# Half loads in 4 KB pieces, early weights behind the last load, a fourth place for outgoing rows: one change to a linear-attention and mixture-of-experts kernel

## The chip, the cores and the metric

The kernel runs on one NeuronCore of one Trainium2 chip. A core has a matrix engine (TensorE, PE in the profile, with its weight loads as PEld), a vector engine (VectorE, DVE), a scalar engine (ScalarE, ACT), a general engine (GpSimd, POOL) and a queue processor without arithmetic (SyncE, SP). Sixteen DMA engines move data between the chip's memory and the core's on-chip memory; SP, ACT and POOL each hand them transfers from a queue of their own, and each of these engines takes its instructions strictly in order. The metric is the device time of one execution in microseconds (us), lower is better.

## The reference

Two stages. The first is linear attention with decay over 4 batches, 8 heads, 768 positions and head dimension 64, with a state carried from block to block. Its output, 3072 token rows of 512, goes to a mixture of experts with one expert of eight for each token.

```python
def _attn_ref(q, k, v, lam):
    ...
    for b in range(nb):
        sl = slice(b * block, (b + 1) * block)
        qb, kb, vb = (q[:, :, sl], k[:, :, sl], v[:, :, sl])
        intra = np.einsum('bhic,bhjc->bhij', qb, kb) * Dmask[None]
        intra = np.einsum('bhij,bhjd->bhid', intra, vb)
        inter = np.einsum('bhid,bhde->bhie', qb * lam_pow[None], kv_state)
        out[:, :, sl] = intra + inter
        kb_dec = kb * rev_pow[None]
        kv_state = lam_block[None, :, None, None] * kv_state + np.einsum('bhsd,bhse->bhde', kb_dec, vb)

def _moe_ref(x, modality_id, w_gate, modality_bias, w1, w2):
    ...
    logits = x @ w_gate + modality_bias[modality_id]
    e_idx = np.argmax(logits, axis=1)
    ...
    for e in range(E):
        mask = e_idx == e
        h = np.maximum(x[mask] @ w1[e], 0.0)
        out[mask] = gate_w[mask, None] * (h @ w2[e])
    return out.astype(np.float32)
```

## The kernel before

**Attention.** The 768 positions of a batch are cut into 6 chunks of 128, so there are 24 chunks (`NC` = 6, `B` = 4). Two chunks make a half (`HB` = 2): one load of 2 MB brings keys and queries by columns, and values and keys by rows, for both chunks and all heads (`load_half`, L177). There are 12 halves and three buffers for them (`LOADS`). On the host `qkv` is laid out so that everything one partition needs of a half is one run of 16 KB (L882). The first half is loaded as four parts (L68, L90), the decay tables `dk` between them (L84, both from SP), so that chunk 0 can begin.

The loop over `g` (L696) is a pipeline written by hand. In round `g` stand: the scaled queries and keys of chunk g+1 (`prepare`, DVE, L200 and L205), the scores of chunk g (PE L220, masked on DVE at L223), the outputs of chunk g-1 (PE L258 and L269), the state update of chunk g (PE L235) and the token rows of chunk g-2 (`tokens`, L274: PE L281 turns them, ACT L282 copies them into `xn`, ACT's queue stores `xn` to the memory tensor `xs` at L283, DVE L285 sums the router's logits). `xn` has three places, so the copy of chunk n waits until the store of chunk n-3 has landed. A half's load is handed over in round g when the buffer of three halves before is free, that is after the outputs of that half's second chunk.

**Routing.** After each batch DVE ranks the tokens (`route`, `route_places`), and POOL scatters their numbers into the list `inv` (`write_slots`, L355), one write of 128 entries for each chunk. From the first two batches (`SOON`) two tiles of 256 tokens are chosen early (`early_list`, called at g = `early` = 14, with a matmul at L365 that needs the token count `ohsum`). Their list entries are read at g = 18 (`fetch_idx`, L500, waits until the scatters have landed), and their weights `raw1` (`fetch_w1`, L525) and `raw2` (`fetch_w2`, L531) follow in rounds 18 and 20, in four pieces of 512 KB each, all on SP's queue.

**Experts.** A wide tile has 256 tokens; weights, rows and hidden values are split into a high and a low part (`split`, L482 on ACT and L483 on DVE) and multiplied in three products (L548 to L552). A thin tile has 64 tokens and is computed unsplit (L578, L600). The order is: early tile 0 (`run(0)`), early tile 1 with both thin tiles (`run_early(1)`), then ten wide tiles. A weight load carries a condition: when the expert is that of the tile before, SP hands it over, but it moves nothing. In `run(0)` the number and place of all later tiles are worked out once the last tokens are routed (`late_list`); SP then reads register values and list entries of the later tiles (`get_idx`), and the second early tile's `raw2` comes after those in SP's order (L796). In `run_early` the rows of the first later wide tile are turned (`turn_rows`, L541) between the turns and products of the thin tiles.

**What sets the order.** The program's order is the basis, and a planner places the instructions of each engine by its own estimate of time. `behind(later, first)` adds a wait, with `wait=False` only an order. SP takes everything in turn: a register load or transfer that waits holds up all that stands behind it.

Of the kernel before, what the change touches and what calls it, by code (L numbers as in the profile page):

```python
# [6 lines left out]
F32 = mybir.dt.float32  # L7
# [8 lines left out]
P = 128  # L16
B, H, S, D = 4, 8, 768, 64
NP = H // 2
NC = S // P
HB = 2  # L20
LOADS = 3
N = B * S
E, DM, F = 8, 512, 1024
KC, FC = DM // P, F // P
TT = 256
# [13 lines left out]
def linear_attention_moe(tc, qkv, lam, modality, wg, mbias, w1, w2, out):  # L39
    nc = tc.nc  # L40
    with ExitStack() as ctx:
# [10 lines left out]
        def behind(later, first, wait=True):  # L52

            info = (mybir.DependencyInfo(mybir.DependencyClass.Sync, mybir.DependencyReason.DATA) if wait else
                    mybir.DependencyInfo(mybir.DependencyClass.NoSync, mybir.DependencyReason.SCHED_ONLY))
            tc.add_manual_dep(later.ins, first.ins.name, info, reason="order")
# [4 lines left out]

        def load_tile():

            return work.tile([P, HB, 4, H * D], F32, name="load", bufs=LOADS)

        first = load_tile()
        for part in (slice(0, 2), slice(2, 4)):
            nc.sync.dma_start(out=first[:, 0, part], in_=qkv[0, 0][:, 0, part])  # L68
        busy = const.tile([P, DM], BF16, name="busy")
        nc.vector.memset(busy, 0.0)  # L70
        tab = const.tile([H, 2 * P], F32, name="tab")
# [9 lines left out]

        dk = const.tile([P, 2, NP, P], F32, name="dk")
        for hl in range(2):
            tables = nc.sync.dma_start(  # L84
                out=dk[:, hl],
                in_=bass.AP(tensor=tab_d.tensor, offset=tab_d.offset + hl * 2 * P,
                            ap=[[1, P], [4 * P, NP], [1, P]]),
            )
        for part in (slice(0, 2), slice(2, 4)):
            ld = nc.sync.dma_start(out=first[:, 1, part], in_=qkv[0, 0][:, 1, part])  # L90
            behind(ld, tables, wait=False)
            tables = ld

# [81 lines left out]
        nc.vector.memset(ohsum, 0.0)  # L175

        def load_half(g):  # L177
            b, h = divmod(g, NC // HB)
            t = load_tile()
            behind(nc.sync.dma_start(out=t, in_=qkv[b, h]), tables, wait=False)  # L180
            return t

        halves = {0: first}

        def loaded(g):

            t = halves[g // HB][:, g % HB]
            kt, qt = (t[:, i].rearrange("p (a t) -> p a t", a=NP) for i in range(2))
            return kt, qt, t[:, 2], t[:, 3]

# [82 lines left out]

        def tokens(g, xt, lg):  # L274
            c = g % NC
            xn = work.tile([P, NP, P + E], F32, name="xn", bufs=3)
            for hf in range(2):
                xp = ps.tile([P, 2, 256], F32, name="x", bufs=2)
                for j in range(2):
                    p = hf * 2 + j  # L280
                    nc.tensor.matmul(xp[:, j, : P + E], xt[:, p, :], iw[:, p, :], start=True, stop=True)  # L281
                copies.append(nc.scalar.copy(out=xn[:, 2 * hf : 2 * hf + 2, :], in_=xp[:, :, : P + E]))  # L282
            nc.scalar.dma_start(out=xs[g * P : (g + 1) * P, :].rearrange("t (p d) -> t p d", p=NP),  # L283
                                in_=xn[:, :, :P])
            logits.append(nc.vector.tensor_reduce(out=lg[:, c, :], in_=xn[:, :, P:].rearrange("p q e -> p e q"),  # L285
                                                  axis=AX, op=ALU.add))
# [204 lines left out]
        def item(lst, row, i):  # L491
            return lst[0:1, row, i : i + 1] if isinstance(i, int) else lst[0:1, row, i]

        def fetch_idx(lst, i, idx, cols=TT):
            vr = nc.sync.value_load(item(lst, 1, i), min_val=0, max_val=E * CAP)
            if cols < TT:
                for p in range(0, P, cols):
                    nc.sync.dma_start(out=idx[p : p + cols, 0, :], in_=inv[bass.ds(vr, cols), 0:2])
                return
            nc.sync.dma_start(out=idx, in_=inv[bass.ds(vr, TT), 0:2].rearrange("(t p) c -> p t c", t=2))  # L500

        def groups(cols):

# [28 lines left out]
                if after is not None:  # L532
                    behind(ld, after)

        def turn_rows(cols, before=None):
            for i in range(2):
                tp = ps.tile([P, 2, TT], F32, name="x", bufs=2)
                for j in range(2):
                    kc = 2 * i + j
                    for t, m in groups(cols):  # L540
                        mm = nc.tensor.transpose(out=tp[:, j, t * P : t * P + m],  # L541
                                                 in_=xg[t][:m, kc * P : (kc + 1) * P], identity=ident[:m, :m])
                        if before is not None:
                            behind(mm, before, wait=False)
                split(tp[:, :, :cols], xh[i][:, :, :cols], xl[i][:, :, :cols])
# [150 lines left out]
        for g in range(0, ng + 2):  # L696
            if 1 <= g < ng - 1:
                st0[g + 1] = prepare(g + 1)
            if g == 2:
                routing_constants()  # L700
            if g < ng:
                st1[g], masked = scores(g)
            if g == 0:
                spread_powers()
                keep_busy(14)
                behind(nc.sync.dma_start(out=iw[:, :, P:], in_=wg), tables, wait=False)
                for i in range(1, LOADS):
                    halves[i] = load_half(i)
                for i in range(2):
                    st0[i] = prepare(i, masked)  # L710
            if 1 <= g <= ng:
                st2[g - 1], passed = outputs(g - 1, st1.pop(g - 1), from_state(g - 1, st0[g - 1][0]))
            if g < ng:
                passed = carry(g, st0[g][1]) or passed

            if g >= HB and g % HB == 0 and LOADS - 1 + g // HB < ng // HB:
                halves[LOADS - 1 + g // HB] = load_half(LOADS - 1 + g // HB)
            if g >= 2:
                b, c = divmod(g - 2, NC)
                if c == 0:  # L720
                    lgs[b] = work.tile([P, NC, E], F32, name="lg", bufs=2)
                tokens(g - 2, st2.pop(g - 2), lgs[b])
                if routed is not None:
                    slots = route_places(*routed)
                    routed = None
                if c == NC - 1:
                    routed = (b, *route(b, lgs.pop(b)))

            few = 2 if early <= g < early + 3 else 1
            write_slots(slots[:few], passed)  # L730
            slots = slots[few:]

            if g == early:
                exA, nA = early_list()
                er, _ = fetch_regs(listA, 0, True)
            elif g == early + 4:
                for i in range(EARLY):
                    fetch_idx(listA, i, idxA[i])
                fetch_w1(er, {})
            elif g == early + 6:  # L740
                fetch_w2(er, {})
            elif g == ng - 2:
                fetch_rows(idxA[0], TT, SOON * S, after=fades[-1])
            elif g == ng:
                split(raw1[0], w1h[0], w1l[0], late=True)
                turn_rows(TT)
            elif g == ng + 1:
                for i in range(1, 4):
                    split(raw1[i], w1h[i], w1l[i], late=True)
                fetch_w1(*fetch_regs(listA, 1, False))  # L750
                fetch_rows(idxA[1], TT, SOON * S)
# [11 lines left out]
        def regs(n):  # L763
            return fetch_regs(*tiles[n][1:], False)
# [21 lines left out]
        def run(n):  # L786
            idx = idxs.get(n) or get_idx(n)
            begun, turned = wide(tail, before)
            if n == 0:
                write_slots(route_places(*routed, begun))  # L790
                late_list(exA, nA)
            if n + 1 < fixed_ones:
                ahead = range(EARLY, wides + 1) if n == 0 else range(n + 2, min(n + 3, fixed_ones))
                for m in ahead:
                    idxs[m] = get_idx(m)
                fetch_w2(*regs(n + 1))  # L796
                turn_rows(TT, turned)
                for m in ahead:
                    gathered = rows_of(m)
                for i in range(4):  # L800
                    split(raw1[i], w1h[i], w1l[i])
                if n + 2 < fixed_ones:
                    fetch_w1(*regs(n + 2), gathered)
            second(idx)

        def run_early(n):
# [10 lines left out]
            fetch_w1(*regs(wides))  # L817
            other, mm = thin_first(xf[1], both[0])
            hnt = [thin_turn(hn, mm)]
            turn_rows(TT)  # L820
            gathered = rows_of(wides + 1)
            mm = thin_second(idxs[EARLY], hnt[0], raw2)
            hnt.append(thin_turn(other, mm))
            fetch_w2(*regs(wides))
            before = thin_second(idxs[EARLY + 1], hnt[1], both[1])
            w1h, w1l = parts(F32R)
# [75 lines left out]
```

## Time and profile before

| | us |
|---|---|
| median of three runs | 448.57 (447.22 to 452.23) |
| the profiled execution's own time | 450.08 |
| its span, from the first to the last instruction | 448.3 |
| PE busy in the span | 416.4 |
| DVE busy | 247.6 |
| ACT busy | 188.1 |
| POOL busy | 105.6 |

The span has 9446 instructions. Busy time of PE is modelled from pipelined matmuls, so it says where PE had work, not that it ran at its peak. Its average hides two very different stages: attention runs until about 130 us, the experts from there to the end. "PEclk" in the windows is the share of its full clock that TensorE was granted; "DMA share" is the mean busy share of the 16 DMA engines, and can read a little over 1. In the timeline a bracket gives the idle time of an engine before the instruction and what ended it. The chain of waits is followed back from the last instruction.

### The profile page before, as it was taken

Reading aid. Unit: us, or ns where it says so; the run is one execution under the profiler, and the core shown is the slowest. Engines: PE = TensorE matmul, PEld = TensorE weight load, DVE = VectorE, ACT = ScalarE, POOL = GpSimd, SP = SyncE. Lnnn points to the kernel's source line nnn. Section 1 sums busy time; section 2 is a strip of 40 time slices with the busy share of each in tenths; the row PEclk is TensorE's granted clock in tenths of the full one; section 3 lists DMA queues with packets and bytes.
Section 4 is the critical chain, followed back from the end, with each engine's and each line's share of the span. In section 5 each row is a group of like instructions: output and inputs, shape, how many; then the busy total and the mean of one; then the engine's idle time right before and its main releaser. Section 6 shows DMA issues by size and latency. Waiting matters only on the chain.

```text
span 448.3 us, 9446 instructions
## 1 busy us (share of the span) xinstructions
PE 416.4 (93%) x3635; PEld 364.9 (81%) x3636; DVE 247.6 (55%) x481; ACT 188.1 (42%) x298; POOL 105.6 (24%) x110
## 2 busy tenths in 40 slices
PE   8899699899789998989999999999999999999980
PEld 4688588788669896759898999999998989898960
DVE  4686566756547946027837282919090919182510
ACT  1223133233158514134746363637272819182510
POOL 3110134431450343103221111313122221201010
PEclk9999889999898999999999999999999999999995
DMA  4999949778932012741112667530202020100000
GB/s 144 425 362 418 321 134 322 265 258 307 370 109 72 2 52 55 251 176 53 48 48 59 223 215 257 173 109 24 73 9 86 2 94 7 58 25 25 25 29 16
DMA packets 30356, 63.90 MB, mean 143 GB/s; under 512 B 6997, under 2 KB 20701, under 8 KB 28896
## 3 DMA queue, kind: packets, MB, share of 16 engines
q1 hardware_dynamic: 12816, 44.14, 27.7%
q0 software_dynamic: 4800, 12.79, 8.5%
q10 hardware_dynamic: 12688, 6.30, 4.7%
q8 instruction: 30, 0.49, 0.5%
q14 instruction: 22, 0.18, 0.1%
HBM read 91.04 MB, written 14.64 MB: 236 GB/s over the span
## 4 chain that ended last, share of the span: by engine, by line
issue 44%; PE 17%; DMA 16%; DVE 8%; POOL 7%; SPq 3%; ACT 1%; another core or an unknown queue 1%; POOLq 0%; ACTq 0%; DVEq 0%
DMA idx<-inv 4%; PE x L281 4%; POOL out_dram L622 4%; PE s L220 4%; PE o L269 4%; DMA xs<-xn 4%; POOL xg L508 3%; DMA xg<-xs,idx 3%; DMA load<-in_qkv_dram 2%; PE o L258 2%; DVE w1l L483 2%; DMA inv<-pay,sloti 2%; PE kv L235 2%; SPq L525 1%; DMA dk<-tab_d 1%
## 5 line engine op out<-in xcount | busy, mean ns | idle before, releaser
L548 PE MATMUL s<-xh,w1h 128*128 128x256 f32 x384 | 108.6, 283 | 0.8 <-issue 0.8
L551 PE MATMUL s<-xl,w1h 128*128 128x256 f32 x384 | 108.4, 282 | 0.0
L552 PE MATMUL s<-xh,w1l 128*128 128x256 f32 x384 | 108.2, 282 | 0.0
L483 DVE TENSOR_TENSOR w1l<-raw,w1h 128x1024 fp32r<-128x1024 f32 x48 | 58.0, 1220 | 75.1 <-ACT w1h L482 73.1
L551 PE MATMUL o<-w2l,hh 128*128 128x512 f32 x192 | 74.8, 390 | 2.0 <-DVE w2l L483 2.0
L548 PE MATMUL o<-w2h,hh 128*128 128x512 f32 x192 | 75.8, 395 | 0.0
L552 PE MATMUL o<-w2h,hl 128*128 128x512 f32 x192 | 74.9, 390 | 0.0
L548 PEld LDWEIGHTS s<-xh,w1h 128*128 128x128 f32 x384 | 72.6, 189 | 1.8 <-issue 1.4
L551 PEld LDWEIGHTS s<-xl,w1h 128*128 128x128 f32 x384 | 72.8, 190 | 0.4
L552 PEld LDWEIGHTS s<-xh,w1l 128*128 128x128 f32 x384 | 72.7, 189 | 0.1
L483 DVE TENSOR_TENSOR w2l<-raw,w2h 128x1024 fp32r<-128x1024 f32 x48 | 58.4, 1219 | 2.7 <-ACT w2h L482 2.2
L482 ACT CAST w1h<-raw 128x1024 fp32r<-128x1024 f32 x48 | 49.7, 1052 | 22.2 <-PE s L551 22.2
L482 ACT CAST w2h<-raw 128x1024 fp32r<-128x1024 f32 x48 | 49.8, 1041 | 0.1
L508 POOL DMA_INDIRECT xg<-xs,idx x20 | 27.7, 1383 | 83.7 <-PE x L541 80.0
L567 DVE SCALAR_TENSOR_TENSOR hl<-s,hh 128x512 fp32r<-128x512 f32 x48 | 32.9, 686 | 24.6 <-ACT hh L566 24.6
L621 ACT ACTIVATE y<-o,idx 128x512 f32<-128x512 f32 x20 | 13.8, 689 | 76.1 <-PE o L552 42.8
L622 POOL DMA_INDIRECT out_dram<-y,idx x20 | 21.4, 1068 | 101.0 <-ACT y L621 101.0
L551 PEld LDWEIGHTS o<-w2l,hh 128*128 128x128 f32 x192 | 36.1, 188 | 9.7 <-DVE w2l L483 2.5
L552 PEld LDWEIGHTS o<-w2h,hl 128*128 128x128 f32 x192 | 36.0, 188 | 7.5
L548 PEld LDWEIGHTS o<-w2h,hh 128*128 128x128 f32 x192 | 36.0, 188 | 7.1
L271 ACT COPY xt<-o 128x256 f32<-128x256 f32 x48 | 17.8, 372 | 54.8 <-PE o L269 47.9
L566 ACT ACTIVATE hh<-s 128x512 fp32r<-128x512 f32 x48 | 28.5, 594 | 23.2 <-PE s L552 13.7
(192 smaller groups left out, 505.4 us busy)
## 6 DMA issues: line engine op xcount, KB each, us to landing
raw<-in_w_dram SPq DMA_DIRECT2D x104, 512.0 KB
load<-in_qkv_dram SPq DMA_DIRECT2D x11, 2048.0 KB
xs<-xn ACTq DMA_DIRECT2D x24, 256.0 KB
load<-in_qkv_dram SPq DMA_DIRECT2D x4, 512.0 KB
w1h<-in_w_dram SPq DMA_DIRECT2D x4, 512.0 KB
w1l<-in_w_dram SPq DMA_DIRECT2D x4, 512.0 KB
inv<-pad SPq DMA_DIRECT2D x2, 392.0 KB
inv<-pad SPq DMA_DIRECT2D x2, 384.0 KB
```

What stands on the lines that cost most here:

```text
L220: nc.tensor.matmul(sps[hl][:, p, :], kt[r, p, :], qt[r, p, :], start=True, stop=True)
L269: mm = nc.tensor.matmul(op[half][place(p, hl), i, :], vt[:, (2 * p + hl) * D : (2 * p + hl + 1) * D], pts[hl][:, p, :], start=(c == 0 and ...
L281: nc.tensor.matmul(xp[:, j, : P + E], xt[:, p, :], iw[:, p, :], start=True, stop=True)
L482: cp = nc.scalar.copy(out=hi, in_=src)
L483: df = nc.vector.tensor_tensor(out=lo, in0=src, in1=hi.bitcast(F32), op=ALU.subtract)
L508: last = nc.gpsimd.indirect_dma_start(out=(to or xg)[t][:m], out_offset=None, in_=xs[:rows, :], in_offset=bass.IndirectOffsetOnAxis(ap=idx ...
L548: mm = nc.tensor.matmul(out, ah, bh, start=first, stop=False)
L551: nc.tensor.matmul(out, ah, bl, start=False, stop=False)
L552: return nc.tensor.matmul(out, al, bh, start=False, stop=last)
L566: act = nc.scalar.activation(out=hh[i], in_=hp, func=AF.Relu)
L567: nc.vector.scalar_tensor_tensor(out=hl[i], in0=hp, scalar=0.0, in1=hh[i].bitcast(F32), op0=ALU.max, op1=ALU.subtract)
L622: sc = nc.gpsimd.indirect_dma_start(out=out, out_offset=bass.IndirectOffsetOnAxis(ap=idx[:, t, 0:1], axis=0), in_=y, in_offset=None, bound ...
```

## The change

Five edits. The half's tile and its source are turned round, so that the four kinds of data (keys and queries by columns, values and keys by rows) are outermost: a partition's share of a half becomes four runs of 4 KB, 512 KB apart, and of the four first parts two runs of 2 KB instead of one of 4 KB. The first of the two tables is handed over by ACT's queue. `xn` gets a fourth place. The early list is made one round later; the early tile's list entries are ordered behind the last load of a half, and its weights wait until that load has landed. In `run(0)` the second early tile's `raw2` stands ahead of the later tiles' list entries; in `run_early` the second part of the row turns stands behind the products of the first thin tile, and the gather after it.

```diff
-            return work.tile([P, HB, 4, H * D], F32, name="load", bufs=LOADS)
+            return work.tile([P, 4, HB, H * D], F32, name="load", bufs=LOADS)
+
+        def source(g):
+            return qkv[divmod(g, NC // HB)].rearrange("x p c f -> p x c f")
...
-            nc.sync.dma_start(out=first[:, 0, part], in_=qkv[0, 0][:, 0, part])
+            nc.sync.dma_start(out=first[:, part, 0], in_=source(0)[:, part, 0])
...
-            tables = nc.sync.dma_start(
+            tables = (nc.scalar, nc.sync)[hl].dma_start(
...
-            ld = nc.sync.dma_start(out=first[:, 1, part], in_=qkv[0, 0][:, 1, part])
+            ld = nc.sync.dma_start(out=first[:, part, 1], in_=source(0)[:, part, 1])
...
-            b, h = divmod(g, NC // HB)
             t = load_tile()
-            behind(nc.sync.dma_start(out=t, in_=qkv[b, h]), tables, wait=False)
+            ld = nc.sync.dma_start(out=t, in_=source(g))
+            behind(ld, tables, wait=False)
+            loads.append(ld)
             return t
...
-            t = halves[g // HB][:, g % HB]
+            t = halves[g // HB][:, :, g % HB]
...
-            xn = work.tile([P, NP, P + E], F32, name="xn", bufs=3)
+            xn = work.tile([P, NP, P + E], F32, name="xn", bufs=4)
...
-        def fetch_idx(lst, i, idx, cols=TT):
+        def fetch_idx(lst, i, idx, cols=TT, after=None):
...
-            nc.sync.dma_start(out=idx, in_=inv[bass.ds(vr, TT), 0:2].rearrange("(t p) c -> p t c", t=2))
+            ld = nc.sync.dma_start(out=idx, in_=inv[bass.ds(vr, TT), 0:2].rearrange("(t p) c -> p t c", t=2))
+            if after is not None:
+                behind(ld, after, wait=False)
...
-        def turn_rows(cols, before=None):
-            for i in range(2):
+        def turn_rows(cols, before=None, part=range(2)):
+            for i in part:
...
-            if g == early:
+            if g == early + 1:
                 exA, nA = early_list()
                 er, _ = fetch_regs(listA, 0, True)
             elif g == early + 4:
                 for i in range(EARLY):
-                    fetch_idx(listA, i, idxA[i])
-                fetch_w1(er, {})
+                    fetch_idx(listA, i, idxA[i], after=loads[-1])
+                fetch_w1(er, {}, loads[-1])
             elif g == early + 6:
-                fetch_w2(er, {})
+                fetch_w2(er, {}, loads[-1])
...
                 ahead = range(EARLY, wides + 1) if n == 0 else range(n + 2, min(n + 3, fixed_ones))
+                if n == 0:
+                    fetch_w2(*regs(n + 1))
                 for m in ahead:
                     idxs[m] = get_idx(m)
-                fetch_w2(*regs(n + 1))
+                if n > 0:
+                    fetch_w2(*regs(n + 1))
...
             hnt = [thin_turn(hn, mm)]
-            turn_rows(TT)
-            gathered = rows_of(wides + 1)
+            turn_rows(TT, part=(0,))
             mm = thin_second(idxs[EARLY], hnt[0], raw2)
             hnt.append(thin_turn(other, mm))
+            turn_rows(TT, mm, part=(1,))
+            gathered = rows_of(wides + 1)
             fetch_w2(*regs(wides))
...
-        "qkv": c(_np.stack([cols(kr), cols(inputs["q"]), rows(vr), rows(kr)], axis=4)),
+        "qkv": c(_np.stack([cols(kr), cols(inputs["q"]), rows(vr), rows(kr)], axis=2)),
```

More of the change, by code (lines that the diff above doesn't have):

```diff
@@ L177, in load_half @@
         def load_half(g):
-            b, h = divmod(g, NC // HB)
             t = load_tile()
-            behind(nc.sync.dma_start(out=t, in_=qkv[b, h]), tables, wait=False)
+            ld = nc.sync.dma_start(out=t, in_=source(g))
+            behind(ld, tables, wait=False)
+            loads.append(ld)
             return t
-        halves = {0: first}
+        halves, loads = {0: first}, []
         def loaded(g):
-            t = halves[g // HB][:, g % HB]
+            t = halves[g // HB][:, :, g % HB]
             kt, qt = (t[:, i].rearrange("p (a t) -> p a t", a=NP) for i in range(2))
```

## The prediction

> **What bounds the kernel now.** I read the page first, then a table of windows, then the chain of waits in order of time, and last the timeline around each gap of PE.
>
> ```profile
> span 448.3 us, 9446 instructions
> ...
> DMA packets 30356, 63.90 MB, mean 143 GB/s; under 512 B 6997, under 2 KB 20701, under 8 KB 28896
> ```
>
> The windows run from the end of one chunk's outputs to the end of another's: span, busy time of PE, PEld, DVE, ACT, POOL, PEclk, DMA share, GB/s.
>
> ```profile
> 46.88:58.71 11.83, 7.50 (x88) 6.57 (x85) 7.97 (x27) 2.60 (x9) 2.19 (x2) 0.71 0.80 267
> 58.71:79.10 20.39, 20.39 (x334) 18.00 (x330) 13.68 (x33) 7.73 (x21) 7.79 (x8) 1.00 0.77 257
> 79.10:99.20 20.10, 18.22 (x288) 15.48 (x284) 14.48 (x53) 5.87 (x16) 7.97 (x8) 1.00 0.77 259
> 99.20:112.85 13.65, 13.18 (x207) 11.25 (x203) 7.70 (x23) 4.79 (x13) 1.55 (x2) 1.00 0.90 307
> 112.85:120.50 7.65, 4.45 (x44) 3.97 (x44) 4.70 (x14) 1.15 (x3) 3.22 (x4) 0.78 1.04 408
> 20.50:46.88 26.38, 25.30 (x408) 22.06 (x410) 18.79 (x39) 6.40 (x18) 3.52 (x4) 1.00 1.00 382
> 192.00:194.00 2.00, 2.00 (x18) 1.25 (x15) 0.00 (x0) 0.31 (x1) 0.00 (x0) 1.00 1.03 420
> ...
> 204.26:436.20 231.94, 230.86 (x1514) 211.50 (x1512) 125.63 (x136) 119.45 (x156) 47.03 (x39) 1.00 0.24 79
> ```
>
> From 204 us to the end PE is full at full clock; nothing in this change removes work there, so what is gained earlier should arrive at the end whole. Undisturbed attention is the second row: chunks 9 to 13, five chunks in 20.39 us, 4.1 us each, PE full. Against this pace two stretches stand out: the first row, one chunk in 11.83 us, and the fifth, with 3.20 us of idle PE and a clock of 0.78. The chain names what they wait for.
>
> ```profile
> 32.17 16.67 DMA xs<-xn
> ...
> 93.12 7.74 DMA inv<-pay,sloti
> 102.05 0.53 SPq L525
> 103.26 10.95 DMA load<-in_qkv_dram
> ```
>
> A store of 256 KB took 16.67 us, one small scatter 7.74, and a half 10.95. The store is 512 rows of 512 B, 32 for each DMA engine; a half is 128 runs of 16 KB (11 such loads give 1408 of the 30356 − 28896 = 1460 packets of 8 KB and more). At 420 GB/s an engine moves 16 KB in 16384 / (420000/16) = 0.62 us, and 32 times that is 20 us: the store's time is about that of one 16 KB run of a load ahead of each of its rows.
>
> **The change, part by part.** Gains are negative.
>
> *Stores and the fourth place.*
>
> ```profile
> 48.94 0.67 ACT L282 COPY xn<-x 128x272 f32<-128x272 f32 x2 [5.98 <-DMA xs<-xn]
> 49.38 1.19 PE L281 MATMUL x<-iw,xt 128*128 128x136 f32 x8 [2.08 <-ACT xn L282]
> ```
>
> ACT's copy waits 5.98 us for the store of three chunks before, PE behind it; the window's idle PE is 11.83 − 7.50 = 4.33 us, and it then runs on a reduced clock. One chunk at 4.1 us and some 0.4 of routing matmuls would have done: the stretch costs 7.3 us. With 4 KB runs the store should take about 32 × 0.16 = 5 us plus its latency, and with four places it must land only four chunks later, some 16 us. Ends: −7.7 (idle 4.33 and 0.29 of 11.83 in clock) and −4.0 (runs of 4 KB don't help; the next copy waits some 3 us for that same store). I take −7.3, since both remedies stand behind it. The Trainium skill (TensorE: Matmul & The Clock Gate, Part 1) says the clock halves after an idle window of about 3.4 us and is back after one busy window. By that the clock would cost about 1.7 here, the term 6.0 and the sum 1.3 less; the row's 0.71 over 11.83 us is more than that, and I go by the row.
>
> *What is late next: the halves.*
>
> ```profile
> 71.10 8.33 SPq L180 DMA_DIRECT2D load<-in_qkv_dram  x2
> ...
> 81.16 0.69 DVE L200 TENSOR_TENSOR qd<-load,pq 128x512 f32<-128x512 f32 x1 [1.22 <-DMA load<-in_qkv_dram]
> ...
> 82.98 0.18 PE L365 MATMUL x<-ohsum,onesb 128*128 128x8 bf16 x1 [1.25 <-DVE ohsum L350]
> ```
>
> A half handed over at 71.10 is used at 81.16, 10.06 us, after a wait of 1.22; two chunks take 8.2. So halves are just too late at the full pace, by about 1 us each, and the stretch from 46.88 hides that now for halves 5 to 7 because PE stands. I add +2. Ends: 0, and +6 if these three wait 2 us each. The runs of 4 KB themselves: the window at 192 is weight loads in 4 KB runs, 420 GB/s, so rate alone costs nothing. Against it, a load now shares each engine with stores that used to lag (0.52 MB of rows for 2.1 MB, a fifth of 5 us, +1 us); for it, its last run ends 0.5 us sooner. Per load I take 0, ends −1.5 and +1.5. Handing over 512 runs instead of 128 costs SP, which mostly waits, about the 0.2 us between these two issues:
>
> ```profile
> L180 SPq DMA_DIRECT2D load<-in_qkv_dram x11: 327/336/1007, 9.7 to 103.3; - x11
> L283 ACTq DMA_DIRECT2D xs<-xn x24: 520/521/577, 19.6 to 136.6; - x24
> ```
>
> *Start.*
>
> ```profile
> 11.49 1.48 DVE L223 TENSOR_TENSOR pt<-s,dk 128x512 f32<-128x512 f32 x2 [5.17 <-DMA dk<-tab_d]
> ...
> 21.04 1.16 PE L220 MATMUL s<-load 64*128 64x128 f32 x16 [0.72 <-DMA load<-in_qkv_dram]
> ```
>
> The second table is handed over one issue (0.5 us) earlier: −0.3; ACT, which now waits for the table's memory copy, has nothing else due before PE's powers. If that cover went, it would cost the issue, 0.5. Half 1 lands with half 2 queued behind it in long runs; short ones should finish it sooner: −0.7, the wait shown. The first parts in 2 KB runs hide behind the matmuls that keep PE busy. Together −1.0, ends −1.2 and +0.5.
>
> *Early list a round later.* L365 waited 1.25 us in PE's queue, with the next scores behind it, because DVE's count was not done. A round later it is: −1.2, ends −1.25 and 0. Some 20 small DVE operations move along; DVE has room there (14.48 of 20.10 us busy), or else they cost what they did.
>
> *List entries and weights behind the last load.*
>
> ```profile
> 105.51 9.58 SPq L531 DMA_DIRECT2D raw<-in_w_dram  x4
> 114.31 0.69 DVE L200 TENSOR_TENSOR qd<-load,pq 128x512 f32<-128x512 f32 x1 [5.33 <-DMA load<-in_qkv_dram]
> 116.05 0.72 PE L235 MATMUL kv<-load,kd 128*64 128x64 f32 x16 [3.21 <-DVE state L244]
> 130.63 1.05 ACT L482 CAST w1h<-raw 128x1024 fp32r<-128x1024 f32 x1
> ```
>
> SP waited for the scatters, handed over the list reads and two weight pieces, and only then the last half (103.26), about 4 us after chunk 17's outputs (99.20) freed its buffer; then 4 MB of weights shared the DMA engines. PE lost 3.20 idle and about 0.22 × 7.65 = 1.7 of clock, 4.9. Now the load goes first and alone and should wait like the other halves: −4.0, ends −4.9 and −1. The new wait holds eight weight pieces and nothing else on SP until the experts begin. Cover: handed over at about 99.5, the half lands near 109.5; the weights' 4 MB take 10 us at the fifth row's 408 GB/s, and the first cast, now at 130.63, then comes near 125.7, 6 us later. Were that gone, late weights would cost PE the difference one for one.
>
> *Second early tile's weights.*
>
> ```profile
> SPq L517 <- DVE many L477: 18.6, 1, 18.6
> ```
>
> ```profile
> 169.17 3.14 SPq L531 DMA_DIRECT2D raw<-in_w_dram  x4
> ```
>
> ```profile
> 176.22 0.50 PE L551 MATMUL o<-w2l,hh 128*128 128x512 f32 x1 [2.04 <-DVE w2l L483]
> ...
> 191.72 1.94 PE L578 MATMUL s<-w1h,xf 128*64 128x256 f32 x14 [0.17 <-DMA w1h<-in_w_dram]
> ...
> 200.66 3.67 PE L600 MATMUL o<-w1l,hnt 128*64 128x256 f32 x32 [0.78 <-DVE hnt L589]
> ```
>
> SP stood 18.6 us at the later tiles' registers, and `raw2` behind it went out at 169.17, so DVE's split was late and PE waited 2.04. Handed over first, that wait goes. But 15 us later the thin tile's weights arrive just in time (0.17), and these still hang on the later list: PE would come to them 2 us too early. They gain only the time of `raw2`'s four issues and register reads on SP, where those count. I take the middle, −1.0, ends −2.0 and 0.
>
> *Row turns in `run_early`.* Half of the turns fill the wait of 0.78: −0.7, ends −0.8 and +0.5 (the gather behind them leaves later, covered by a full PE).
>
> Sum: −7.3 + 2.0 − 1.0 − 1.2 − 4.0 − 1.0 − 0.7 = −13.2. The profiled execution took 450.08 us, so 436.9; the median of the runs, 448.57, lies 1.5 lower and would give 435.4. I forecast **436**.
>
> **The rivals.**
>
> *The halves stay the bound.* DMA share is 1.00 from 20.50 to 46.88. Then +2 becomes +6 and the last half keeps 2 of its 5: 436 + 4 + 1 = 441. For: waits of 1 us at every half already. Against: share 0.77 in the undisturbed stretch.
>
> *Halves come sooner.* If short runs take 1.5 us off each landing, the +2 goes, the last half keeps no wait (1 us), and the stretch from 79.10 to 99.20, four chunks in 20.10 us against 16.4 at the pace, loses what of its 3.7 isn't counted yet, 2.5: 436 − 2 − 1 − 2.5 = 430. Against: the halves shown took 10.06 and 10.95 us, and rows now claim their turns among the runs.
>
> *Runs don't matter to stores.* If an engine doesn't take turns by run, stores stay at 16 us and the scatter at 7.7; only the place and the orders help: 436 + 3.3 + 1 = 440.
>
> *Loads in pieces are slower: the other side.* A partition's four runs lie 512 KB apart, where 16 KB were contiguous. From half 5 on seven halves wait; each microsecond of landing beyond about 10 costs 7. At 10 + 13/7 = 11.9 us the gain is gone. At half the rate the flow, some 6 of the 10 us, doubles: 16 us, 436 + 42 = 478; at 13.5 us, 460. Against: the weights' runs, 4 KB too, at 420 GB/s. The Trainium skill (DMA: Bandwidth & Descriptors, Latency and other measured facts) gives 207 GB/s for a row pitch of 512 KB between partitions. Here partitions are 4 KB apart and only the runs of one partition so far, and no row of this trace shows it.
>
> **How the numbers follow.** Forecast 0.55 (431 to 441 by its own bounds), halves the bound 0.17, halves sooner 0.13, stores unmoved 0.08, slower loads 0.07. The range 428 to 443 leaves out the slower loads and thin tails, under 0.2. About 1% is what a measurement tells from no change, here below 444.1 or above 453.1: faster 0.87 (all but the slower loads and the bad end of the second case), same 0.07, slower 0.06.
>
> **What would show it.** Right: stores landing in 5 to 8 us and no wait of ACT on them; clock 1.00 from 46 to 58; the last half handed over within 1 us of its buffer, PE's gap before it under 1.5 us; no wait at L365; weights landed 5 us before the first cast; PE's wait for `w2l` gone and one of 0.5 to 2 us at the thin tile's `w1h`; the rest from there as long as now, 232 us. Wrong: halves landing in over 11 us, DVE waits of 2 us and more at each, or a late first cast.

## The result, and the profile after

The changed kernel takes 433.29 us, the median of four runs (431.24 to 433.84; a fifth execution took 434.76), against 447.89 us for the kernel before, run on the same chip (four runs, 445.23 to 452.23). The ratio is 0.9693 with a 95% interval of 0.9636 to 0.975: some 3.1% faster. The forecast was 436 in a range of 428 to 443.

The profiled execution of the changed kernel took 431.24 us, the fastest of its runs, and that of the kernel before 450.08, one of the slower ones. The two traces therefore differ by 18.8 us where the medians differ by 14.6, and a comparison of stages between them shows some 4 us too much. These are the head of the changed kernel's page, its row of clocks in 40 slices and its packets.

```profile
span 429.2 us, 9451 instructions
...
PE 411.1 (96%) x3635; PEld 361.6 (84%) x3636; DVE 246.9 (58%) x481; ACT 188.2 (44%) x298; POOL 107.3 (25%) x110
...
PEclk9999999999999999999999999999999999999995
...
DMA packets 35092, 63.90 MB, mean 149 GB/s; under 512 B 6997, under 2 KB 20701, under 8 KB 35040
```

PE is busy 5.3 us less than before (416.4 there), though it has the same work: those are the stretches on a reduced clock, and in this row of clocks no slice but the last is below 9. Only 52 packets of 8 KB and more are left of 1460, so the runs did become short.

The windows of both traces, cut at the same places of the program, show where the time went. Columns as in the prediction: span, busy time of PE, PEld, DVE, ACT, POOL, then PEclk, DMA share, GB/s. First the kernel before: chunk 21, from there to the second early tile's first product, on to the thin tiles, on to the first later wide tile, and the rest. (Its rows for chunk 8, chunks 9 to 13, 14 to 17 and 18 to 20 stand in the prediction.)

```profile
112.85:122.13 9.28, 6.08 (x78) 5.43 (x80) 5.99 (x16) 1.15 (x3) 4.38 (x6) 0.82 1.03 392
122.13:159.83 37.70, 35.92 (x298) 31.79 (x293) 27.73 (x85) 21.61 (x36) 14.11 (x13) 0.95 0.21 61
159.83:185.70 25.87, 23.72 (x154) 20.82 (x152) 9.79 (x27) 7.89 (x11) 7.88 (x8) 1.00 0.30 85
185.70:204.26 18.56, 17.26 (x146) 10.70 (x144) 5.60 (x8) 6.11 (x9) 1.99 (x2) 1.00 0.53 206
204.26:448.30 244.04, 230.86 (x1514) 211.50 (x1512) 125.63 (x136) 119.45 (x156) 47.98 (x39) 0.98 0.23 76
```

Now the changed kernel, from chunk 8 on. Its chunk 7 ends at 46.89, against 46.88 before.

```profile
46.89:52.28 5.39, 5.03 (x86) 4.42 (x83) 5.25 (x22) 1.45 (x5) 1.00 (x1) 1.00 1.06 355
52.28:73.16 20.88, 20.88 (x335) 18.34 (x332) 14.86 (x36) 7.81 (x21) 9.09 (x9) 1.00 0.90 304
73.16:91.09 17.93, 17.93 (x287) 15.58 (x284) 14.27 (x53) 6.06 (x16) 7.78 (x8) 1.00 0.92 301
91.09:104.07 12.98, 12.98 (x215) 11.53 (x211) 11.48 (x35) 4.79 (x13) 3.09 (x4) 1.00 0.96 295
104.07:108.37 4.30, 4.30 (x79) 3.81 (x76) 2.02 (x5) 1.51 (x4) 3.13 (x5) 1.00 1.05 394
108.37:144.91 36.54, 34.43 (x298) 30.17 (x293) 27.72 (x85) 21.41 (x35) 13.79 (x13) 1.00 0.35 121
144.91:168.24 23.33, 23.33 (x153) 20.89 (x152) 9.85 (x27) 7.74 (x11) 9.89 (x8) 1.00 0.29 84
168.24:185.66 17.42, 16.73 (x147) 11.33 (x145) 5.55 (x8) 6.13 (x9) 1.99 (x2) 1.00 0.62 233
185.66:429.20 243.54, 230.81 (x1514) 211.50 (x1512) 125.44 (x137) 119.33 (x156) 47.98 (x39) 0.98 0.24 76
```

Row against row, changed minus before, and beside it the term of the prediction that belongs there:

| stretch | measured, us | forecast, us |
|---|---|---|
| start to the end of chunk 7 | 0.0 | -1.0 |
| chunk 8 (stores, fourth place) | -6.4 | -7.3 |
| chunks 9 to 13 (late halves) | +0.5 | +2.0 |
| chunks 14 to 17 (early list) | -2.2 | -1.2 |
| chunks 18 to 21 (last half, weights) | -0.7 - 5.0 = -5.7 | -4.0 |
| to the second early tile | -1.2 | 0 |
| second early tile (`raw2`) | -2.5 | -1.0 |
| thin tiles (row turns) | -1.1 | -0.7 |
| the rest | -0.5 | 0 |
| sum | -19.1 | -13.2 |

The two large terms are where the prediction put them. From chunk 9 to chunk 21 PE is busy in every microsecond of the window. DVE still waits for halves, as the changed kernel's timeline of DVE says (start, duration, instruction, and in brackets the idle time before it and what ended it):

```profile
57.20 0.69 DVE L209 TENSOR_TENSOR kd<-load,dk 128x512 f32<-128x512 f32 x1 [2.66 <-DMA load<-in_qkv_dram]
...
65.73 0.69 DVE L204 TENSOR_TENSOR qd<-load,pq 128x512 f32<-128x512 f32 x1 [0.87 <-DMA load<-in_qkv_dram]
...
91.27 0.69 DVE L204 TENSOR_TENSOR qd<-load,pq 128x512 f32<-128x512 f32 x1 [0.48 <-DMA load<-in_qkv_dram]
```

The queue of SP around the last half, in the same kernel, shows the new order: half, list entries, then the weights as soon as the half has landed.

```profile
91.15 0.37 SPq L182 DMA_DIRECT2D load<-in_qkv_dram  x1
91.81 1.93 SPq L504 DMA_DIRECT2D idxA<-inv  x2
99.64 2.78 SPq L531 DMA_DIRECT2D raw<-in_w_dram  x4
102.62 3.02 SPq L537 DMA_DIRECT2D raw<-in_w_dram  x4
```

The half goes out 0.1 us after chunk 17's outputs (91.09) have freed its buffer, and lands before 99.64, in less than 8.5 us; before, it was some 4 us late and took 11.05 (103.26 to 114.31). The weights are handed over by 105.6, and the first cast of them comes at 116.87, so the new wait on SP is covered.

### The profile page after: what moved, and what is told of

Read it like the earlier page. It is cut to its first block, busy times and chain, and to the rows that moved or that the text cites. A ratio compares the mean times of both kernels' runs of the same rounds, so it can differ in the third digit from the quotient of the medians.

```text
span 429.2 us, 9451 instructions
## 1 busy us (share of the span) xinstructions
PE 411.1 (96%) x3635; PEld 361.6 (84%) x3636; DVE 246.9 (58%) x481; ACT 188.2 (44%) x298; POOL 107.3 (25%) x110
## 4 chain that ended last, share of the span: by engine, by line
issue 43%; PE 28%; DMA 13%; POOL 7%; DVE 3%; SPq 2%; ACT 1%; POOLq 0%; ACTq 0%
DMA load<-in_qkv_dram 6%; PE s L224 5%; PE x L285 4%; PE o L273 4%; POOL out_dram L628 4%; DMA idx<-inv 4%; DMA xg<-xs,idx 3%; POOL xg L514 3%; PE o L262 2%; PE o L554 2%; PE o L558 2%; PE o L557 2%; PE s L558 2%; PE kv L239 2%; PE s L557 2%
## 5 line engine op out<-in xcount | busy, mean ns | idle before, releaser
L514 POOL DMA_INDIRECT xg<-xs,idx x20 | 29.7, 1484 | 83.7 <-PE x L547 80.1
L628 POOL DMA_INDIRECT out_dram<-y,idx x20 | 20.3, 1013 | 100.9 <-ACT y L627 100.9
```

What stands on the lines that cost most here:

```text
L514: last = nc.gpsimd.indirect_dma_start(out=(to or xg)[t][:m], out_offset=None, in_=xs[:rows, :], in_offset=bass.IndirectOffsetOnAxis(ap=idx ...
L628: sc = nc.gpsimd.indirect_dma_start(out=out, out_offset=bass.IndirectOffsetOnAxis(ap=idx[:, t, 0:1], axis=0), in_=y, in_offset=None, bound ...
```

## The experiments

Times are medians with their range; the ratio is to the kernel before on the same chip in the same session. The kernel before took 449.09 us in the first session (long runs again, three places, short runs alone, weights free again), 449.03 in the second (neither, second early tile late, early list sooner, both turns) and 446.98 in the third (ordered without the wait, two places). All start from the changed kernel but the one that says otherwise.

### Long runs again

```diff
-            return work.tile([P, 4, HB, H * D], F32, name="load", bufs=LOADS)
+            return work.tile([P, HB, 4, H * D], F32, name="load", bufs=LOADS)
...
-        "qkv": c(_np.stack([cols(kr), cols(inputs["q"]), rows(vr), rows(kr)], axis=2)),
+        "qkv": c(_np.stack([cols(kr), cols(inputs["q"]), rows(vr), rows(kr)], axis=4)),
```

> The changed kernel with the half laid out in runs of 16 KB again, all else as changed. Theory A (DMA engines take turns by run, so short runs are what lets stores and scatters land): each store again takes about 16 us; with four places the copy of a later chunk still waits some 3 us, the scatters come late again, so of the 14.6 us gained 3 to 6 are lost: 436 to 439 us, DVE's waits on halves as before the change. Theory B (the fourth place and the orders do it, the runs are beside the point): 433 us, within 1 of the changed kernel.

Measured: 433.18 us (431.96 to 434.19), ratio 0.9629 (0.9601 to 0.9656), the same time as with short runs. This kernel's timelines of ACT and DVE:

```profile
48.26 0.68 ACT L286 COPY xn<-x 128x272 f32<-128x272 f32 x2 [0.62 <-DMA xs<-xn]
```

```profile
56.75 0.76 DVE L209 TENSOR_TENSOR kd<-load,dk 128x512 f32<-128x512 f32 x1 [2.77 <-DMA load<-in_qkv_dram]
```

With four places the copy waits only 0.62 us for a store even when loads move in runs of 16 KB. Halves come as late as with short runs (2.77 beside 2.66). Once there are four places, the length of a run is beside the point.

### Three places

```diff
-            xn = work.tile([P, NP, P + E], F32, name="xn", bufs=4)
+            xn = work.tile([P, NP, P + E], F32, name="xn", bufs=3)
```

> The changed kernel with three places for outgoing rows again. Theory A: stores land in 5 to 8 us among 4 KB runs, three places give 8 us and more, so no wait of ACT on a store over 1 us and 433 to 434 us. Theory B: the stores are as slow as ever, ACT waits 5 us for one near chunk 8, the clock drops and 6 to 7 us come back: 440 us.

Measured: 435.56 us (434.65 to 436.65), ratio 0.9699 (0.9669 to 0.9728). ACT's timeline has a short wait, but the chain of waits (start, duration, what) holds a store that is far from short:

```profile
49.23 0.68 ACT L286 COPY xn<-x 128x272 f32<-128x272 f32 x2 [0.19 <-DMA xs<-xn]
```

```profile
35.67 13.48 DMA xs<-xn
```

So short runs without the fourth place also take away the wait of 6 us, yet not because a store takes 5 us now: this one takes 13.48. The time lies above theory A's 433 to 434. The store that had been late before is the one ahead of it. In the kernel before it took 16.67 us and was needed 10.8 us after it was handed over (32.17 to 48.94 - 5.98 in the prediction's rows). Here it is handed over at 31.83, and the copy that needs its place starts at 43.86 without waiting for it, so it took 12.0 us at most: at least 4.6 us less.

### Neither short runs nor a fourth place

```diff
-            xn = work.tile([P, NP, P + E], F32, name="xn", bufs=4)
+            xn = work.tile([P, NP, P + E], F32, name="xn", bufs=3)
...
-        "qkv": c(_np.stack([cols(kr), cols(inputs["q"]), rows(vr), rows(kr)], axis=2)),
+        "qkv": c(_np.stack([cols(kr), cols(inputs["q"]), rows(vr), rows(kr)], axis=4)),
```

> The changed kernel with runs of 16 KB and three places, all other edits kept. The runs alone (443.91) and the runs taken away (433.18) say that either remedy frees ACT of the store. Theory C (one of the two is enough, each is spare beside the other): without both ACT waits 4 to 6 us near chunk 8, the clock drops, 439 to 441 us. Rival (the wait near chunk 8 depended on the scatters and weights too, which stay mended here): 434 to 436 us.

Measured: 442.87 us, ratio 0.9857 (0.983 to 0.9884). One of its six runs, at 2278.82 us, stands far apart from the others (440.96 to 443.96) and is left out of the ratio. ACT's timeline and the window of chunk 8:

```profile
48.26 0.67 ACT L286 COPY xn<-x 128x272 f32<-128x272 f32 x2 [6.03 <-DMA xs<-xn]
```

```profile
46.10:57.87 11.77, 7.40 (x84) 6.47 (x81) 7.96 (x27) 2.50 (x8) 2.18 (x2) 0.72 0.78 260
```

The stall of the kernel before is back, to the tenth: 6.03 beside 5.98 us, 11.77 beside 11.83 us, a clock of 0.72 beside 0.71. The four combinations together, with the other edits in place:

| | three places | four places |
|---|---|---|
| runs of 16 KB | 442.87 | 433.18 |
| runs of 4 KB | 435.56 | 433.29 |

Either remedy brings most of the gain, 7.3 or 9.7 us, and the second adds 2.3 at most, or nothing. The times come from three sessions; by the ratios to the kernel before, 0.9699 with short runs and three places and 0.9693 with both remedies, the fourth place adds even less to short runs. One is the other's spare.

### Short runs alone, on the kernel before

```diff
-            return work.tile([P, HB, 4, H * D], F32, name="load", bufs=LOADS)
+            return work.tile([P, 4, HB, H * D], F32, name="load", bufs=LOADS)
...
-        "qkv": c(_np.stack([cols(kr), cols(inputs["q"]), rows(vr), rows(kr)], axis=4)),
+        "qkv": c(_np.stack([cols(kr), cols(inputs["q"]), rows(vr), rows(kr)], axis=2)),
```

> The kernel before with the halves in 4 KB runs and nothing else of the change. Theory A: the wait of ACT on a store near chunk 8 is gone (6 us), the wait at L365 and the one for the last half stay: 441 to 442 us against 448. Theory B: no gain, 447 to 448 us. Third possibility, that a half in pieces lands later: 450 us and more.

Measured: 443.91 us (443.69 to 445.3), ratio 0.9884 (0.9856 to 0.9911). No wait of ACT for a store is left at chunk 8, and the last half is as late as ever, as DVE's timeline and the chain show:

```profile
108.09 0.69 DVE L203 TENSOR_TENSOR qd<-load,pq 128x512 f32<-128x512 f32 x1 [5.97 <-DMA load<-in_qkv_dram]
```

```profile
96.25 11.74 DMA load<-in_qkv_dram
```

Short runs cure the first stall and do nothing for the second, which is a matter of order. That the wait of PE for the token count would stay was wrong: the early list is made in round 14 here, as before, and the count's matmul (at 76.30, L368) doesn't wait. The gain is 5.2 us, not the 6 to 7 of theory A. Chunks 14 to 17 take 18.74 us in this kernel, against 20.10 before:

```profile
73.68:92.42 18.74, 18.19 (x288) 15.52 (x284) 14.39 (x53) 5.87 (x16) 7.68 (x8) 1.00 0.82 269
```

### Weights free again

```diff
-                    fetch_idx(listA, i, idxA[i], after=loads[-1])
-                fetch_w1(er, {}, loads[-1])
+                    fetch_idx(listA, i, idxA[i])
+                fetch_w1(er, {})
...
-                fetch_w2(er, {}, loads[-1])
+                fetch_w2(er, {})
```

> The changed kernel with the early tile's list entries and weights no longer ordered behind the last load. Theory A (the weights and the wait for the scatters in front of the last load cost 5 us at chunk 21): DVE waits 4 to 5 us for the last half, the clock drops, 437 to 438 us. Rival (short runs and an earlier scatter already let the last half through): no more than 1 us lost, 433 to 434 us.

Measured: 439.79 us (438.17 to 444.52), ratio 0.982 (0.976 to 0.988). SP's timeline in this kernel, then its window of chunk 21:

```profile
91.52 1.59 SPq L504 DMA_DIRECT2D idxA<-inv  x2
93.30 0.35 SPq L531 DMA_DIRECT2D raw<-in_w_dram  x1
93.83 0.38 SPq L182 DMA_DIRECT2D load<-in_qkv_dram  x1
94.41 2.10 SPq L531 DMA_DIRECT2D raw<-in_w_dram  x3
96.70 11.96 SPq L537 DMA_DIRECT2D raw<-in_w_dram  x4
```

```profile
104.18:113.14 8.96, 6.08 (x80) 5.41 (x80) 5.99 (x16) 1.14 (x3) 4.37 (x6) 0.81 1.04 407
```

The window is nearly that of the kernel before (9.28 us, PE 6.08, clock 0.82). Against the first experiment, of the same session, the missing order costs 6.6 us. (That kernel has long runs, which made no difference there.) The half goes out behind the list entries and one weight piece and is used only at 105.32, as DVE's timeline says:

```profile
105.32 0.69 DVE L204 TENSOR_TENSOR qd<-load,pq 128x512 f32<-128x512 f32 x1 [5.24 <-DMA load<-in_qkv_dram]
```

### Ordered, but without the wait for landing

```diff
-                    behind(ld, after)
+                    behind(ld, after, wait=after not in loads)
```

> The changed kernel with the early weights ordered behind the last load but without the wait for its landing. Theory E (what cost 5 us at chunk 21 is mainly 4 MB of weights beside the last half): DVE waits 3 to 4 us for the last half, 436 to 437 us. Rival (it was SP, held by the list entries in front of the load): 433 to 434 us, and the wait for the landing is spare.

The edit stands in both weight fetches. Measured: 432.56 us (430.92 to 433.62), ratio 0.9705 (0.9656 to 0.9754). SP's timeline:

```profile
90.78 0.38 SPq L182 DMA_DIRECT2D load<-in_qkv_dram  x1
91.44 1.91 SPq L504 DMA_DIRECT2D idxA<-inv  x2
93.54 6.93 SPq L531 DMA_DIRECT2D raw<-in_w_dram  x4
```

Three weight pieces are handed over here while the last half is on its way, and DVE takes that half up at 99.54 without waiting:

```profile
99.54 0.69 DVE L204 TENSOR_TENSOR qd<-load,pq 128x512 f32<-128x512 f32 x1
```

The order carries the gain; the wait for landing adds nothing that could be measured. Against the run with free weights the half goes out 3.05 us sooner (90.78, 93.83) and lands in under 8.8 us instead of 11.5. How much of those 2.7 us is the piece ahead of it, and how much the four handed over behind it before it landed, these runs don't separate: with the order, three were handed over beside it, and SP held the fourth until 100.13.

### Second early tile's weights late again

```diff
-                if n == 0:
-                    fetch_w2(*regs(n + 1))
...
-                if n > 0:
-                    fetch_w2(*regs(n + 1))
+                fetch_w2(*regs(n + 1))
```

> The changed kernel with the second early tile's second weights again behind the later tiles' list entries. As the prediction has it, PE waits 2 us for w2l again but meets its thin weights 1 us later: 434 to 434.5 us against 433.3. Rival, by the landmarks of the two traces (2.7 us gained between the starts of the second early tile and of the thin tiles, 1.1 more after): nothing is given back, 435.5 to 436.5 us.

Measured: 434.65 us (433.85 to 439.04), ratio 0.9686 (0.9648 to 0.9724). PE's timeline:

```profile
162.00 0.50 PE L557 MATMUL o<-w2l,hh 128*128 128x512 f32 x1 [1.08 <-DVE w2l L487]
...
177.68 3.87 PE L584 MATMUL s<-w1h,xf 128*64 128x256 f32 x30 [2.10 <-DMA w1h<-in_w_dram]
```

Both waits are there, 1.08 us for the split weights and 2.10 for the thin tile's. The changed kernel's profile has neither, but its median is only 1.4 us lower, which the spread of these runs doesn't tell from nothing.

### Early list a round sooner

```diff
-            if g == early + 1:
+            if g == early:
```

> The changed kernel with the early list made in round 14 again. As predicted: PE waits 1.2 us at the count and the chunk after it starts later by that: 434.3 to 434.8 us. Rival (the wait came from DVE's wait for a half, and is hidden otherwise): 433 to 433.5 us.

Measured: 436.94 us (435.1 to 439.87), ratio 0.973 (0.9697 to 0.9763). The time is 3.6 us above the changed kernel's, from another session, and the intervals of the ratios overlap. The wait of 1.25 us that the edit was to remove does not come back in this profile, so if the later list gains something, the reason given for it is not the one. The window of chunks 14 to 17 bounds what it can gain in these chunks:

```profile
72.63:91.44 18.81, 18.24 (x287) 15.52 (x284) 14.38 (x53) 5.87 (x16) 7.77 (x8) 1.00 0.82 266
```

It is 18.81 us long, 0.9 more than in the changed kernel's profile. Other variants with the list in round 15 take 17.94 (ordered without the wait) to 18.49 us (neither remedy).

### Both row turns ahead of the first thin product

```diff
-            turn_rows(TT, part=(0,))
+            turn_rows(TT)
+            gathered = rows_of(wides + 1)
...
-            turn_rows(TT, mm, part=(1,))
-            gathered = rows_of(wides + 1)
```

> The changed kernel with both row turns ahead of the first thin product again. As predicted: PE waits 0.8 us for the hidden values' copy before the second thin product, 433.8 to 434.2 us. Rival (the copy is late anyway, DVE being the one that sets it): 433.2 to 433.4 us.

Measured: 436.5 us (433.94 to 437.65), ratio 0.9712 (0.9681 to 0.9743). PE's timeline:

```profile
186.98 3.67 PE L606 MATMUL o<-w1l,hnt 128*64 128x256 f32 x32 [0.78 <-DVE hnt L595]
```

The wait of 0.78 is back, beside one of 0.35 at 181.35, where the changed kernel has two of 0.35, at 177.01 and 182.05. So splitting the turns gains 0.4 us of PE's waits; the whole time can't settle a few tenths.

### Two places, with three lengths of run

To time the stores under a full load stream, `xn` gets only two places, so that ACT's copy shows when a store landed. One execution each, with runs of 4 KB, 16 KB (as in the first experiment) and 2 KB:

```diff
-            xn = work.tile([P, NP, P + E], F32, name="xn", bufs=4)
+            xn = work.tile([P, NP, P + E], F32, name="xn", bufs=2)
```

and for 2 KB besides, chunks ahead of positions in memory:

```diff
...
-            return qkv[divmod(g, NC // HB)].rearrange("x p c f -> p x c f")
+            return qkv[divmod(g, NC // HB)].rearrange("x c p f -> p x c f")
...
-        "qkv": c(_np.stack([cols(kr), cols(inputs["q"]), rows(vr), rows(kr)], axis=2)),
+        "qkv": c(_np.stack([cols(kr), cols(inputs["q"]), rows(vr), rows(kr)], axis=2).transpose(0, 1, 2, 4, 3, 5)),
```

> The changed kernel (runs of 4 KB) with two places for outgoing rows, so that ACT's copy waits for the store of two chunks before and its landing can be read off. Theory A (an engine takes turns by run: 32 rows each behind one run of 4 KB, 0.16 us): stores land in 5 to 8 us while halves flow, waits short. Theory D (a row waits for some 10 KB of loads whatever the run, as the 13.48 us of a store in the run with three places says): 12 to 14 us between 20 and 50 us, ACT waits 5 us and more there.

> The same with runs of 16 KB. Both theories: about 16 us for a store while halves flow, as in the kernel before (16.67). If it were 13 us or less, the length of the runs would do nothing at all for the stores.

> The same with runs of 2 KB (the two chunks of a half laid apart as well). Theory A: stores land in 3 to 6 us. Theory D: 10 to 13 us, little under those of 4 KB.

Measured: 445.14 us (4 KB), 445.1 (16 KB) and 439.5 (2 KB). ACT's timelines, first 4 KB (with the copy for the next store as well), then 16 KB, then 2 KB; a store and the copy that needs its place:

```profile
31.95 0.52 ACTq L287 DMA_DIRECT2D xs<-xn  x1
...
42.73 0.67 ACT L286 COPY xn<-x 128x272 f32<-128x272 f32 x2 [5.35 <-DMA xs<-xn]
...
49.10 0.67 ACT L286 COPY xn<-x 128x272 f32<-128x272 f32 x2 [4.46 <-DMA xs<-xn]
```

```profile
31.76 0.52 ACTq L287 DMA_DIRECT2D xs<-xn  x1
...
48.34 0.67 ACT L286 COPY xn<-x 128x272 f32<-128x272 f32 x2 [11.15 <-DMA xs<-xn]
```

```profile
35.75 0.52 ACTq L287 DMA_DIRECT2D xs<-xn  x1
...
44.87 0.85 ACT L286 COPY xn<-x 128x272 f32<-128x272 f32 x2 [0.74 <-PE x L285]
```

The first store, handed over at about 32 us, takes 10.8 us beside runs of 4 KB (31.95 to 42.73) and 16.6 beside runs of 16 KB. Beside runs of 2 KB it is done within 9.3 us (31.91 to a copy at 41.17 that waits for DVE and not for it). The next store takes 13.3 us beside runs of 4 KB (35.78 to 49.10). Beside runs of 16 KB it is done within 14.5 (35.60 to a copy at 50.14 that doesn't wait), and beside 2 KB within 9.1 (35.75 to 44.87, where the copy waits for PE). So a store is faster beside shorter runs, but not in proportion: 4 KB take a third off the first store, and for the second the runs show no clear difference between 4 and 16 KB. Neither theory fits throughout. Theory A's 5 to 8 us for 4 KB is wrong. Theory D's 12 to 14 us is near there, but its 10 to 13 us for 2 KB is too long, and how far below 9.1 us a store falls at 2 KB can't be read here. Later, with mostly one half on its way, stores take about 8 us in all three (8.4 with 16 KB, 74.18 to 82.59).

## Why the prediction was right, and where it wasn't

Sign, size and places are right: both stalls named from the chain are gone, the rest runs as before (243.5 beside 244.0 us from the first later wide tile on), and 433.29 lies in the range. The sum is too small by 5.9 us against the profiled pair and by 1.4 against the medians. That it comes so near the medians is in part luck: in the pair, two terms are too hopeful by 1.9 us together and the others too cautious by 7.8, while the pair itself shows some 4 us too much.

**Stores and the fourth place.** This step failed in its reason: "With 4 KB runs the store should take about 32 × 0.16 = 5 us plus its latency." Stores take 10.8 to 13.5 us in that stretch. The rule of one run ahead of each row gives 20 us for 16 KB, where 16.6 were measured, and for 4 KB less than half of what was measured: the time doesn't shrink in proportion to the run, and the runs did not show what else takes part. The term held since the other remedy stood behind it, as the prediction said, and since the store that matters was short enough for three places (10.8 us with two places, 12.0 at most with three). The lower end of its gain, 4.0, was too low: with long runs and four places the next copy waited 0.62 us for that store and not some 3. The rival "runs don't matter to stores" had 16 us for a store, which is too long too, and its price was wrong: long runs with four places lose nothing (433.18), where it gave 440.

**The size of that stall.** -6.4 instead of -7.3, because chunk 8 without any wait for a store takes 5.39 us and not the 4.5 that were assumed. The clock's share can now be priced: the kernel with neither remedy needs 11.77 - 5.39 = 6.38 us more there, and its PE is idle for 4.37 - 0.36 = 4.01 more, which leaves 2.4 us for the reduced clock (0.72 in that row). The Trainium skill (TensorE: Matmul & The Clock Gate, Part 1), with half clock until one busy window is over, gave 1.7 as an estimate; the row that the prediction went by gives 0.29 × 11.83 = 3.4. The measurement lies between.

**Late halves.** +2 was mis-sized: +0.5. DVE does wait for halves (2.66, 0.87, 0.48 us), yet PE never did behind it, for DVE prepares a chunk ahead. The prediction took such waits for time that PE loses. It also counted with a landing in about 10 us, where the four halves that DVE waited for in the changed kernel from 57 us on took 10.3, 9.1, 8.4 and 8.3 us. Nor do short runs make halves sooner or later: 83.01 to 91.27 is 8.26 us here, 83.11 to 91.46 is 8.35 with long runs. (The prediction's 0.52 MB of rows beside 2.1 MB of load make a quarter of 5 us and not a fifth; it took that term as 0 all the same.) This ends the rival of slower loads, and that of halves made sooner by short runs. The Trainium skill's 207 GB/s for a row pitch of 512 KB between partitions (DMA: Bandwidth & Descriptors, Latency and other measured facts) is not seen where only a partition's own runs lie so far apart: the changed kernel's rows of attention read 295 to 394 GB/s.

**Start.** -1.0 forecast, 0.0 measured. Gained at chunk 2 (0.3 us) and lost by chunk 7.

**Early list.** -2.2 against -1.2 in the pair, and the reason fails. The wait at the token count is gone, but the list put back a round sooner didn't bring it back, and with short runs alone, list unmoved, it is gone too. The four chunks take 18.7 to 18.8 us in those two profiles and 17.9 to 18.5 with the later list, against 20.1 before. So some 1.3 of the 2.2 us go without moving the list, and 0.9 at most are left for the move. In the kernel before, DVE had waited 1.22 us for a half just ahead of the count (81.16 in the prediction's rows); in those two profiles it comes to the count without such a wait. That this wait was the cause is the likely reading, and not tested by itself.

**Weights behind the last half.** -5.7 against -4.0; nothing waits for the last half at all. The reason is right in one half: the order matters (439.79 without it), the wait for landing does not (432.56).

**Second early tile and row turns.** -2.5 and -1.1 against -1.0 and -0.7. The prediction had the thin tile's `w1h` take back 0.5 to 2 us. The profiled run has no wait there, as PE's timeline says:

```profile
171.75 3.89 PE L584 MATMUL s<-w1h,xf 128*64 128x256 f32 x32
```

In the profiles of the variants with three or four places the wait is 1.04 us (long runs), 1.4 (three places), 1.4 (free weights), 1.7 (neither), 1.9 (turns together), 2.1 (late `raw2`), 2.4 (early list) and 0 (order only). With two places it is 0.17, 0.74 and 0 us (4, 16 and 2 KB). Where SP had handed `w1h` over 2.1 to 2.8 us ahead of the thin tile, PE waited 1 us or more; with 3.4 us and more (3.5 in the changed kernel, 164.78 for a start at 168.24) it mostly waited little or nothing. But the kernel with the late `raw2` had 4.1 us and still waited 2.1, so this lead alone doesn't decide. So the forecast wait is there in most of these profiles, each of another kernel, and the changed kernel's own profile is without it. That profile and the one of the kernel ordered without the wait are the two fastest executions of all, 431.24 and 430.92. That the changed kernel's profile was lucky here, and that this wait makes up the spread of the runs, are inferences; no run was made to test them.

**Not foreseen.** The stretch to the second early tile is 1.2 us shorter. Its clock reads 0.95 in the kernel before and 1.00 in the changed one. This is hardly an effect of the change: after the same wait of PE of 0.98 or 0.99 us at the first wide tile, the clock over the ten microseconds around it reads 0.83 in the profiles of five other kernels (short runs alone, long runs, neither, late `raw2`, turns together) and of the kernel before, and 1.00 in those of four others and of the changed kernel.

## What to carry to other kernels

When a copy waits for a store, price one more buffer before reshaping the traffic: a fourth place here did all that shorter runs did, and both together little more. A load that the critical engine needs belongs in front of everything on its queue that waits or that is needed later; a plain order was enough, and a wait for its landing was not needed. A wait of an engine that prepares a chunk ahead is not a loss of the engine behind it; count what PE loses, in PE's own row.

## What the runs showed of the hardware

Beside a stream of loads that keeps the DMA engines full (share 1.00 and more from 20.5 to 46.9 us), a store of 256 KB in rows of 512 B took up to 16.6 us when the loads' runs were 16 KB, 10.8 to 13.5 at 4 KB and 9.3 at most at 2 KB; with mostly one load of 2 MB on its way it took about 8 us whatever the run. The loads themselves were as fast in runs of 4 KB as of 16 KB (8.26 and 8.35 us). And the granted clock does not always answer alike: after the same wait of 0.98 or 0.99 us of PE at the first wide tile, it was 0.83 over the ten microseconds around it in one profile and 1.00 in another, as these two windows show, first of the kernel with both turns together, then of that with the early list.

```profile
118.37:128.37 10.00, 8.24 (x55) 7.82 (x53) 7.63 (x17) 7.17 (x12) 3.36 (x3) 0.83 0.38 111
```

```profile
119.36:129.36 10.00, 7.90 (x63) 7.28 (x61) 8.03 (x18) 7.80 (x13) 3.35 (x3) 1.00 0.38 109
```
